# One more chunk in seven products: a two-stage kernel with its attention batches drawn closer together

## The chip, the cores and the metric

The kernel runs on one core of one Trainium2 chip. A core has engines that run side by side, each through its own list of instructions in order: TensorE (PE, matrix products, with PEld as its weight loads), VectorE (DVE), ScalarE (ACT), GpSimd (POOL) and SyncE (SP, which here only issues DMAs). They hand work to each other through semaphores. Data lies in SBUF (128 partitions), products land in PSUM banks, and sixteen DMA engines move data between memory and SBUF. The metric is the device time of one execution in microseconds; smaller is better.

## The reference

Four batches of linear attention with four heads come first (1088 positions, head size 32). Each query and key is turned into 64 features, all products of 8 by 8 sketch values:

```python
def phi(x):
    a = np.einsum('rd,bhsd->bhsr', S1, x)
    b = np.einsum('rd,bhsd->bhsr', S2, x)
    return np.einsum('bhsi,bhsj->bhsij', a, b).reshape(*x.shape[:-1], r * r)
q_p, k_p = (phi(q), phi(k))
kv = np.einsum('bhsf,bhsd->bhfd', k_p, v)
z = np.sum(k_p, axis=2)
num = np.einsum('bhsf,bhfd->bhsd', q_p, kv)
den = np.einsum('bhsf,bhf->bhs', q_p, z)[..., None] + 1e-06
```

num / den, reshaped to 4352 tokens of 128 values, is the input x of a gated layer with 1536 inner columns:

```python
gate = 1.0 / (1.0 + np.exp(-(x @ w_gate)))
val = x @ w_val
return (gate * val @ w_out).astype(np.float32)
```

All of it is float32. `z`, the sum of the key features over all positions, is what the text calls the feature sums.

## The kernel before, in words

Tokens are cut into eight chunks of 512 and a last one of 256. Weight columns are taken in blocks of 128, twelve for the gate, twelve for the value; w_out has twelve blocks of rows.

**Slots.** The first SECT = 5 chunks are worked in slots, twelve per chunk, numbered from 0 to 59. A slot (`slot`, line 745) does one wave (`w1`, line 667): the products of one gate block and one value block with 512 tokens, on TensorE; a sigmoid on ACT; and, one slot later, the gating product on DVE (`glu`, line 714). Some slots later come the products with w_out (`w2_a`, `w2_b`). Those use a form with seven products of half size where the plain one has eight, which needs sums of tokens (POOL, `token_sums`) and sums of weights. Two PSUM pairs serve the waves by turns, so TensorE can run about two waves ahead of the gating.

**Attention between slots.** Each batch is threaded through the slots by hand. For batches 2 and 3 the list `plan` (line 1468) says before which slot a step is issued: turning the raw keys and queries (`turn_k`, `turn_q`), `begin` (lines 1367 to 1371: sketch products, then the copies below), two outer products (`outer`), two steps of the feature sums (`sum_z`, line 1057), `kv_all`, a query multiplication (`qmult`) with `ndt`, the second query multiplication, and `parts` (line 1393), which ends the batch and makes its tokens ready. `parts` opens with `den_j` (line 1151), a TensorE product that reads the tile B8; a DVE product with A8 follows. Batch 1 goes through the same steps between slots 11 and 22.

**The copies.** `spread` (line 969) writes the compressed queries (cq) to a tile in DRAM called dq, through the ACT queue, and reads them back on the SP queue in repeated form. Six large reads fill QP and BQ: for each half of the tokens one of 576 KB (qp, source rows `[[8 * W1, 2 * R], [0, R]]`, so 16 outermost) and two of 288 KB (bq, source rows `[[0, R], [8 * W1, R]]`, so 8 outermost). Eight small reads of 32 partitions each follow and fill A8 and B8 (lines 991 to 1003, source `[[8 * W1, 32]] + run`). R is 8 and W1 is 288.

**Weights for the section.** `cross_weights` (line 463) prepares sums of weight halves in the tile fw. Its steps have letters, and `PREP` says after which slot each is done: DMAs between partition halves on ACT (v, w, x, y, z) and on SP (within d, e, n), subtractions and additions on DVE (d, e, s, f, g, t, u), one on ACT (n). X loads the section's first tokens, 0 and 2 form their sums on POOL.

**Section.** The last three full chunks and the chunk of 256 tokens follow in `section` (line 1498). There the first product too has seven products for eight, two blocks of columns by 256 tokens and half the depth at a time, with 64 x 64 quarters of TensorE side by side. Eighteen waves of this kind and the last chunk are issued in the order that the string `ORDER` spells out; a planner wrote it. In it P are feature products, W products with w_out, A, S, D and M the copies, sigmoids, additions and gating, Q and T sums on POOL, E and F the end of a chunk, C, Y, Z and O the last chunk. Two pairs of the last slot chunk (HELD) leave their w_out products to the section.

**Loads.** Raw k and q of a batch lie in one tile (`new_kq`), which later serves as BQ; `load_kq(b + 1)` refills it behind the second query multiplication of batch b, through SP.

Of the kernel before, what the change touches and what calls it, by code (L numbers as in the profile page):

```python
# [19 lines left out]
WUB:-2.0 P1:0 T0:1 P1':0 P5:1 P1':1 P5:0 P1:1 WLA:-2.1 Aa:0 P5':0 P5':1 Aa:1 P2':0 P6':0 P6:0 P2:0  # L20
Ac:0 P2':1 P6':1 Ac:1 D1:0 P2:1 P6:1 Sa:0 D1:1 P3:0 P7':0 P3':0 P7:0 T2:1 P7':1 P3:1 Sc:0 D2:0 P7:1
P3':1 Sa:1 P1:2 WUB:-1.0 D2:1 P5:2 P4':0 Sc:1 P1':2 P4:0 P4:1 P1:3 M1:0 P1':3 P4':1 P5:3 P5':2 Aa:2
M1:1 WUB:-1.1 WLA:-1.0 Ac:2 P6':2 WLA:-2.0 M2:1 P2:2 P6:2 Aa:3 P2':2 P5':3 Q0:1 D1:2 P6':3 P2':3
Ac:3 P6:3 P2:3 M2:0 Q1:1 P7':2 P3':2 Sa:3 P7:2 WLA:-1.1 D1:3 Q0:0 Sa:2 P3:2 P1:5 D2:2 P7:3 P3:3 Q2:1
Sc:2 P3':3 P7':3 P5:4 P4:2 T1:1 Sc:3 D2:3 P4':2 P1:4 Q3:1 P1':4 WUA:-2.0 M1:2 P5:5 P5':4 Q1:0 P1':5
P4':3 M2:2 Aa:4 WUA:-2.1 P4:3 Ac:4 Q2:0 P2:4 P6':4 M1:3 WLB:-2.0 P6:4 Q3:0 P2':4 WUA:-1.0 Aa:5 D1:4
WLB:-1.1 WUA:-1.1 P6:5 P5':5 M2:3 EA:-1 P7:4 P6':5 Sa:4 P3:4 P7':4 Q0:3 P3':4 P2:5 Ac:5 D2:4
WLB:-1.0 WUA:1.0 Q0:2 Sc:4 P1:6 P2':5 D1:5 P4':4 P1':6 EB:-1 T3:1 P4:4 P7':5 Sa:5 P3':5 P7:5 Q1:2
M1:4 WUA:1.1 P5':6 Q1:3 P1':7 P5:6 D2:5 Aa:6 P3:5 WLB:1.1 Ac:6 M2:4 P6':6 P2:6 Q2:3 P4:5 P6:6 Sc:5
P4':5 WUA:0.1 Q0:4 D1:6 WUA:0.0 WLB:1.0 Q3:3 P1:7 WLB:0.0 M1:5 P7:6 P3':6 M2:5 Q2:2 Aa:7 P7':6 P3:6  # L30
P2':6 P5:7 Sc:6 Q1:4 D2:6 P6:7 P5':7 P2':7 P6':7 F0:-1 Ac:7 T0:2 WLA:3.0 P2:7 WLA:0.0 P4':6 D1:7
Q3:2 Sa:7 P5':8 P4:6 M2:6 Sa:6 P5:8 WUB:1.1 Q2:4 P3':7 P7':7 M1:6 P3:7 P7:7 Q3:4 P1':8 P1':9 Sc:7
D2:7 P1:9 P1:8 Q0:5 Ac:8 WLA:0.1 WUB:0.0 P5:9 P4':7 Aa:8 M2:7 Q0:6 P4:7 WUB:3.0 WLA:3.1 WUB:1.0 Q1:5
M1:7 WLA:1.0 P6':8 WLA:2.1 P6:8 F1:-1 T2:2 Aa:9 P5':9 WLA:2.0 D1:8 WUB:2.0 WLA:1.1 Ac:9 WUB:3.1 P6:9
Q0:7 P7:8 P6':9 P7':8 P3:8 D1:9 Q1:7 P3':8 P2:9 P2':8 P2':9 D2:8 Q2:5 Sc:8 P3:9 P2:8 P3':9 P7:9 M2:8
Q1:6 Sa:8 P4':8 P7':9 Sc:9 P4:8 WLB:3.0 Q3:5 D2:9 WUA:2.0 WLB:2.0 Sa:9 WUA:2.1 WLB:3.1 M1:8 WUA:4.0
P4:9 Q0:8 M2:9 P4':9 P1:11 WUA:4.1 P1:10 Q1:8 M1:9 P1':10 P1':11 P5:11 P5':10 F2:-1 Q2:7 Aa:10 P5:10
WUA:3.0 F3:-1 Aa:11 WUA:3.1 WLB:5.0 Q3:7 F4:-1 P6:10 P2:10 Ac:10 P6':10 WLB:5.1 Q2:6 P6:11 P5':11
D1:10 WUA:5.0 WLB:4.0 Q0:9 Ac:11 WUA:5.1 P6':11 F5:-1 P7':10 P3':10 T1:2 D1:11 P7:10 P3:10 P2':11
P2':10 Q1:9 Sc:10 D2:10 P2:11 P7:11 Sa:10 P7':11 P3:11 T3:2 M2:10 P4:10 WLA:5.1 Sa:11 Q3:6 P4':10  # L40
WLA:5.0 D2:11 P3':11 WLA:4.0 Q2:8 WLA:4.1 WUB:4.0 M1:10 Sc:11 P4':11 WUB:5.1 EA:0 P4:11 WUB:5.0
M2:11 P1':13 P1:12 EB:0 P1:13 P1':12 M1:11 Q0:11 P5:13 P5:12 Aa:12 P5':13 P5':12 F6:-1 Q0:10 Aa:13
WUB:7.0 WLA:7.0 P6:12 WLA:6.0 Ac:12 Q1:10 P6':12 P6':13 Ac:13 WUB:7.1 P2:12 D1:12 Q2:10 P6:13
WUB:6.0 P2':13 WLA:7.1 F0:0 Q1:11 P7':12 P3:12 D1:13 P7:12 P3':12 Q3:10 WLA:6.1 P2:13 Sc:12 D2:12
P3':13 P2':12 Q2:11 P3:13 P7':13 M2:12 Sa:12 P7:13 P4:12 Q3:11 Sc:13 WLB:6.0 P4':12 D2:13 P1:14
WUA:6.0 Sa:13 Q3:8 WLB:7.1 WUA:6.1 M1:12 P4:13 P5':15 Q2:9 M2:13 P4':13 P1:15 WUA:7.0 P1':14 Q3:9
M1:13 WUA:7.1 WLB:7.0 Aa:14 P5:14 P1':15 Q0:12 F1:0 P5:15 P5':14 Aa:15 F2:0 P6:14 P2':14 Q0:13 Ac:14
P6':14 WLB:10.0 WLB:11.0 WUA:9.1 Q1:12 Ac:15 D1:14 WUA:8.1 P6':15 WUA:10.1 P6:15 F3:0 Q2:12 P7':14
P3':14 D1:15 P7:14 P3:14 P2:14 WUA:9.0 Sc:14 D2:14 WUA:10.0 WLB:11.1 Sa:14 WLB:9.1 WUA:11.0 M2:14
WLB:8.0 P4':14 WLB:9.0 P4:14 F4:0 P7:15 WUA:11.1 M1:14 P7':15 P3:15 WUA:8.0 P1':16 D2:15 P1:16  # L50
P3':15 P5':16 P2':15 F5:0 Sc:15 P5:16 P2:15 Aa:16 P4':15 WUB:9.1 P5':17 WLA:8.1 Sa:15 WUB:8.0
WLA:8.0 Ac:16 WLA:10.1 P6:16 M2:15 Q0:14 P6':16 P4:15 WLA:9.1 WUB:9.0 Q1:13 D1:16 P1':17 P2:16
WLA:9.0 P1:17 M1:15 Q3:12 P3:16 P7':16 Aa:17 P3':16 P7:16 Q0:15 WLA:10.0 P5:17 Sc:16 D2:16 WUB:10.0
WLA:11.1 Q2:13 Ac:17 WLA:11.0 P2':17 M2:16 P6':17 P2:17 Q3:13 EA:1 P4:16 P6:17 WUB:11.0 P2':16 Q1:15
D1:17 P4':16 WLA:12.0 Sa:16 Q1:14 WUB:11.1 WLA:13.0 Sa:17 P3':17 P7:17 M1:16 Q0:16 P7':17 P3:17 C1:1
Sc:17 D2:17 Q1:16 C0:1 C3:1 M2:17 Y:1 Q2:16 C2:1 EB:1 C0:0 Z:1 Q0:17 P4:17 WUA:13.0 WLB:13.1
WUA:12.0 Q2:14 F6:0 WLB:12.0 WUA:12.1 WLB:13.0 WUA:13.1 Q3:16 F0:1 C1:0 Q3:14 C2:0 F1:1 Y:0 C3:0
F2:1 Q2:15 C0:3 Z:0 C1:2 Q3:15 WUB:13.1 P4':17 WLA:13.1 WUB:12.0 M1:17 WUB:13.0 WLA:12.1 F3:1 C1:3
Q1:17 C2:3 F4:1 Y:3 C3:3 Q2:17 WFA:16.0 Z:3 WFA:14.0 Q3:17 WFA:15.0 WFA:16.1 F5:1 WFA:14.1 F6:1
WFA:15.1 WFA:17.0 WFA:17.1 C0:2 EA:2 WFB:15.0 WFB:17.1 WFB:17.0 WFB:16.0 Y:2 WFB:14.0 WFB:15.1 C2:2  # L60
EB:2 C3:2 F0:2 C1:5 C0:5 Z:2 O0:1 C3:5 C2:5 F1:2 Y:5 C0:4 Z:5 C1:4 C2:4 Y:4 C3:4 F2:2 O0:2 O0:3 Z:4
O1:5 O2:2 O2:1 O1:2 O3:3 F3:2 O3:5 O1:3 F4:2 O0:5 O2:0 O3:4 F5:2 O3:0 O1:0 O2:4 F6:2 O2:5 O1:4 O3:2
O0:0 O2:3 O3:1 O1:1 O0:4
# [4 lines left out]
def kernel(  # L68
# [23 lines left out]
    SECT, HELD = 5, 2  # L92
    PREP = (
        (22, "v"),
        (23, "dw"),
        (24, "ex"),
        (25, "s"),
        (26, "n"),
        (30, "f"),
        (32, "g"),  # L100
        (34, "t"),
        (37, "u"),
        (38, "y"),
        (39, "z"),
        (44, "X"),
        (45, "0"),
        (47, "2"),
# [355 lines left out]
    def cross_weights():  # L463
# [8 lines left out]
        (g0, g1), (v0, v1) = (turns(w_sb[:, k]) for k in range(2))  # L472
        (a0, a1), (b0, b1), (c0, c1) = (turns(fw[0][:, k]) for k in range(3))

        def sub(rows, out, x, y, op=ALU.subtract):
            nc.vector.tensor_tensor(out=out[rows], in0=x[rows], in1=y[rows], op=op)

        def cross(eng, out, x, rows):
# [17 lines left out]
            "u": lambda: sub(LO, b1, c1, a1),  # L496
            "y": lambda: cross(nc.scalar, a0, g0, LO),
            "z": lambda: cross(nc.scalar, a1, g1, HI),
            "X": lambda: load_y(0),
            "0": lambda: [x_sum(0, u) for u in (0, 1)],  # L500
            "2": lambda: [x_sum(0, u) for u in (2, 3)],
        }
        moe["prep"] += [(n, steps[k]) for n, ks in PREP for k in ks]

    def weight_sums(n0, n1):
        w = w_sb[:, 2].rearrange("p (n f) d -> p f n d", f=2)[:, :, n0:n1]
        s = ws[:, :, n0:n1]
        a11, a12 = w[:, 0, :, :64], w[:, 1, :, :64]
        a21, a22 = w[:, 0, :, 64:], w[:, 1, :, 64:]
# [935 lines left out]
    for pi in range(2):  # L1445
        outer(1, pi)
        slot(None, 1)
# [308 lines left out]
```

## Time and profile before

| what | value |
|---|---|
| median of three runs | 284.11 us (284.06 to 284.45) |
| profiled execution | 284.32 us, of which the span of its instructions is 282.5 us |
| granted TensorE clock | 1.000 |
| busy: PE, DVE, POOL, ACT | 276.7, 208.3, 179.7, 119.6 us |
| slots (sigmoid of slot 0 to that of slot 59) | 16.7 to 177.4 us |
| 50 to 178 us, busy DVE, POOL, ACT | 94.8, 85.9, 42.2 of 128 us |
| 178 to 253 us, busy DVE, POOL, ACT | 56.3, 56.1, 41.1 of 75 us |
| first den_j product of batch 1, 2, 3 | 71.89, 128.62, 170.31 us |

Positions in time are counted from the first instruction. In a row of instructions the columns are the start, the length, the engine, the line in the kernel, the operation, the output and inputs by their names in the program, and how many were merged. "SPq" and "ACTq" are instructions of an engine's queue that only issue something; a DMA's row gives the issue, and the data lands later. A float32 product shows as two records. For the waits, the engine and line come first, then who ended the wait, the sum in us, how often, and the longest. For stretches of time, the length is followed by each engine's busy time, the clock, the mean busy share of the sixteen DMA engines, and the rate in GB/s.

### The profile page before, as it was taken

Reading aid. Unit: us, or ns where it says so; the run is one execution under the profiler, and the core shown is the slowest. Engines: PE = TensorE matmul, PEld = TensorE weight load, DVE = VectorE, ACT = ScalarE, POOL = GpSimd, SP = SyncE. Lnnn points to the kernel's source line nnn. Section 1 sums busy time; section 2 is a strip of 40 time slices with the busy share of each in tenths; the row PEclk is TensorE's granted clock in tenths of the full one; section 3 lists DMA queues with packets and bytes.
Section 4 is the critical chain, followed back from the end, with each engine's and each line's share of the span. In section 5 each row is a group of like instructions: output and inputs, shape, how many; then the busy total and the mean of one; then the engine's idle time right before and its main releaser. Section 6 shows DMA issues by size and latency. Waiting matters only on the chain.

```text
span 282.5 us, 7859 instructions
## 1 busy us (share of the span) xinstructions
PE 276.7 (98%) x3204; PEld 158.6 (56%) x3204; DVE 208.3 (74%) x339; ACT 119.6 (42%) x232; POOL 179.7 (64%) x234
## 2 busy tenths in 40 slices
PE   8899999999999999999999999999999999999994
PEld 3554433354444444544444444577788888875674
DVE  6986789847687777786768857577788968579462
ACT  3689742322326222443225223666554554452130
POOL 2666674567575668664778765547798988197300
PEclk9999999999999999999999999999999999999999
DMA  7995540674681267376348520200310031003133
GB/s 210 334 372 144 119 157 15 167 155 138 198 182 43 41 179 151 95 151 182 74 130 155 134 45 15 64 0 18 89 25 2 2 71 19 2 21 66 24 64 57
DMA packets 33332, 29.02 MB, mean 103 GB/s; under 512 B 19216, under 2 KB 27728, under 8 KB 33296
## 3 DMA queue, kind: packets, MB, share of 16 engines
q1 hardware_dynamic: 28880, 25.44, 37.0%
q10 hardware_dynamic: 4416, 3.08, 4.2%
q8 instruction: 25, 0.41, 0.6%
q14 instruction: 11, 0.09, 0.1%
HBM read 20.60 MB, written 3.26 MB: 84 GB/s over the span
## 4 chain that ended last, share of the span: by engine, by line
PE 97%; ACT 1%; POOL 0%; DVE 0%; issue 0%
PE wave L682 37%; PE b L530 24%; PE prod L530 23%; PE moeout L574 4%; PE warm L379 2%; PE kvz L1027 1%; PE nps L1385 1%; PE kps L808 1%; PE moeout L530 1%; PE kvz L1014 1%; PE cqps L954 1%; PE nps L1217 0%; PE denj L1156 0%; PE nps L1169 0%; PE dps L1198 0%; ACT asb L925 0%
## 5 line engine op out<-in xcount | busy, mean ns | idle before, releaser
L682 PE MATMUL wave<-xT,w_sb 128*64 128x512 f32 (+2 forms) x436 | 117.5, 589 | 0.1
L530 PE MATMUL prod<-tsum,ws 64*64 64x256 f32 (+1 forms) x348 | 81.1, 379 | 0.0
L690 ACT ACTIVATE sg<-wave 128x512 f32<-128x512 f32 x60 | 35.8, 597 | 89.3 <-PE wave L682 85.2
L520 POOL TENSOR_TENSOR tsum<-g,tsum 128x256 f32<-128x256 f32 x48 | 47.2, 982 | 30.5 <-DVE g L717 30.2
L682 PEld LDWEIGHTS wave<-xT,w_sb 128*64 128x64 f32 (+1 forms) x436 | 40.0, 143 | 46.2 <-issue 35.9
L530 PE MATMUL b<-yt,fw 64*64 64x256 f32 x792 | 63.5, 378 | 0.0
L717 DVE TENSOR_TENSOR g<-wave,sg 128x512 f32<-128x512 f32 x60 | 41.1, 685 | 27.2 <-ACT sg L690 26.4
L530 PE MATMUL prod<-g,w_sb 64*64 64x256 f32 (+2 forms) x234 | 53.7, 377 | 0.0
L520 POOL TENSOR_TENSOR tsum<-g 128x256 f32<-128x256 f32 x48 | 40.4, 842 | 16.8 <-DVE g L717 16.5
L530 PEld LDWEIGHTS prod<-tsum,ws 64*64 64x64 f32 (+1 forms) x348 | 42.2, 135 | 11.0 <-issue 6.8
L530 PEld LDWEIGHTS b<-yt,fw 64*64 64x64 f32 x792 | 41.6, 133 | 9.6 <-DVE b L622 0.7
L1618 POOL TENSOR_TENSOR tsum<-g 128x256 f32<-128x256 f32 x36 | 28.8, 815 | 18.4 <-DVE g L1605 8.9
L530 PE MATMUL prod<-g,ws 64*64 64x256 f32 (+1 forms) x116 | 33.5, 377 | 0.0
L530 PEld LDWEIGHTS prod<-g,w_sb 64*64 64x64 f32 (+1 forms) x234 | 25.7, 135 | 13.6 <-issue 9.8
L530 PE MATMUL prod<-tsum,w_sb 64*64 64x256 f32 (+1 forms) x116 | 33.1, 379 | 0.0
L1618 POOL TENSOR_TENSOR tsum<-g,tsum 128x256 f32<-128x256 f32 x36 | 29.1, 819 | 1.1
L530 PE MATMUL b<-yt,w_sb 64*64 64x256 f32 x216 | 25.7, 377 | 0.0
L622 DVE TENSOR_TENSOR b<-b,s 128x512 f32<-128x512 f32 x18 | 12.5, 696 | 8.2 <-PE b L530 7.6
L1605 DVE TENSOR_TENSOR g<-c,sg 128x512 f32<-128x512 f32 x18 | 15.9, 886 | 3.5 <-PE prod L530 2.6
L530 PEld LDWEIGHTS prod<-g,ws 64*64 64x64 f32 (+1 forms) x116 | 15.6, 135 | 3.9
L530 PEld LDWEIGHTS b<-yt,w_sb 64*64 64x64 f32 x216 | 15.5, 133 | 2.4
L1597 ACT ACTIVATE sg<-b 128x512 f32<-128x512 f32 x18 | 10.8, 598 | 14.4 <-PE b L530 14.0
(162 smaller groups left out, 380.4 us busy)
## 6 DMA issues: line engine op xcount, KB each, us to landing
qp<-dq SPq DMA_DIRECT2D x7, 576.0 KB, 5.3
bq<-dq SPq DMA_DIRECT2D x14, 288.0 KB
kq<-in_k_dram SPq DMA_DIRECT2D x3, 544.0 KB
kq<-in_q_dram SPq DMA_DIRECT2D x3, 544.0 KB
w_in<-in_moe_w_out_dram SPq DMA_DIRECT2D x6, 256.0 KB
yt<-xT SPq DMA_DIRECT2D x12, 128.0 KB
w_in<-in_moe_w_gate_dram SPq DMA_DIRECT2D x5, 256.0 KB, 6.7
w_in<-in_moe_w_val_dram SPq DMA_DIRECT2D x5, 256.0 KB, 4.7
```

The lines of the kernel that those rows point to most:

```text
L379: nc.tensor.matmul(out=t[:, 0, :n], lhsT=x, rhs=r, start=True, stop=True)
L520: nc.gpsimd.tensor_tensor(out=t[:, u], in0=in0, in1=in1, op=ALU.subtract)
L530: nc.tensor.matmul(out=out, lhsT=lhsT, rhs=rhs, start=start, stop=stop, skip_group_check=True)
L574: nc.tensor.matmul(out=moe["acc"][d], lhsT=w_sb[:, 2, j, d], rhs=g[:, jj], start=(j == 0), stop=(j == NJ - 1),)
L622: nc.vector.tensor_tensor(out=out, in0=in0, in1=in1, op=ALU.add)
L682: nc.tensor.matmul(out=wv[d, which, jj * tw + o : jj * tw + o + tp], lhsT=w_sb[:, which, j0 + jj, d], rhs=xT[:, t0 + o : t0 + o + tp], sta ...
L690: nc.scalar.activation(out=sg, in_=wv[:, 0], func=ACTF.Sigmoid)
L717: nc.vector.tensor_tensor(out=g, in0=wv[:, 1], in1=sg, op=MUL)
L808: nc.tensor.matmul(out=ts[pi][32 * g : 32 * g + 32, : NJK * 32], lhsT=sk[rows, :], rhs=kT_of[b][rows, KBASE[g] : KBASE[g] + NJK], start=Tr ...
L1597: nc.scalar.activation(out=sg[:, :, second], in_=two(gc), func=ACTF.Sigmoid)
L1605: nc.vector.tensor_tensor(out=g[:, :, second], in0=two(c2), in1=sg[:, :, second], op=MUL)
L1618: nc.gpsimd.tensor_tensor(out=t[:, out], in0=in0, in1=in1, op=ALU.subtract)
```

## The change

Chunk 4 moves from the slots to the section: SECT is 4, there are 48 slots, and the section has 24 waves of seven-product form and a new ORDER. So that the attention is done in time:

- Batches 2 and 3 have new places: their steps run from before slot 25 to slot 34 and from before slot 37 to slot 46.
- Batch 3's raw k and q are loaded into tiles of their own through the ACT queue, as steps K, P and Q of PREP behind slots 27, 28 and 29; the `load_kq` at the end of a batch is gone.
- `cross_weights` is called between batch 1's outer products, and PREP starts at slot 14. Two of its DVE steps (t, u) have counterparts on POOL (T, U) that take their place.
- The feature sums are two reductions on DVE over eight blocks of positions; the ninth block, of 64 partitions, is added by four more small products in `kv`. The tile z4 of the sums is no longer needed for them.
- A8 and B8 are read by six DMAs of 64 partitions: two for A8 and one for B8 in each half, with `[2 * W1, 2], [8 * W1, 32]` as the source's rows.

```diff
-    SECT, HELD = 5, 2
+    SECT, HELD = 4, 2
     PREP = (
-        (22, "v"), (23, "dw"), (24, "ex"), (25, "s"), (26, "n"), (30, "f"), (32, "g"),
-        (34, "t"), (37, "u"), (38, "y"), (39, "z"), (44, "X"), (45, "0"), (47, "2"),
+        (14, "v"), (15, "w"), (16, "x"), (17, "de"), (19, "s"), (20, "n"), (23, "f"),
+        (24, "y"), (25, "U"), (27, "K"), (28, "P"), (29, "Q"), (32, "g"), (33, "z"),
+        (35, "T"), (34, "X"), (37, "0"), (41, "2"),
     )
...
+            "T": lambda: sub(every, b0, v0, b0, ALU.add, nc.gpsimd),
+            "U": lambda: sub(LO, b1, c1, a1, eng=nc.gpsimd),
...
+        kx = fwp.tile([P, T, D], F32, tag="kx", name="kx")
+        k_t[3] = kx
+        q_t[3] = [fwp.tile([P, T0, D], F32, tag="qx", name="qx")]
+
+        def load_x(n):
+            t0, tn = (0, T) if n < 0 else (2 * q_chk[n][0], 2 * q_chk[n][1])
+            if n == 1:
+                q_t[3].append(sbA.tile([P, tn, D], F32, tag="z4", name="qx1", bufs=1))
+            src, t = (k, kx) if n < 0 else (q, q_t[3][n])
+            nc.scalar.dma_start(
+                out=t,
+                in_=bass.AP(
+                    tensor=src.tensor, offset=src[3, 0].offset + t0 * D, ap=[[T * D, P], [1, tn * D]]
+                ),
+            )
+
+        steps["K"] = lambda: load_x(-1)
+        steps["P"] = lambda: load_x(0)
+        steps["Q"] = lambda: load_x(1)
...
+        d0, d1 = d[0, 0], d[2, 0]
         for x in range(2):
-            for m in range(2):
-                p0 = 64 * x + 32 * m
-                for i, t in enumerate((A8[b], B8[b])):
-                    d0 = d[2 * i + m, 0]
-                    if i == 0:
-                        offset, run = d0.offset + (W1 - WD) * x, [[W1, 2], [1, WD]]
-                    else:
-                        offset, run = d0.offset + W1 * x, [[1, W1]]
-                    put.dma_start(
-                        out=t[p0 : p0 + 32],
-                        in_=bass.AP(tensor=d0.tensor, offset=offset, ap=[[8 * W1, 32]] + run),
-                    )
+            rows = slice(64 * x, 64 * x + 64)
+            for c in range(2):
+                put.dma_start(
+                    out=A8[b][rows, c],
+                    in_=bass.AP(
+                        tensor=d0.tensor,
+                        offset=d0.offset + W1 * c + (W1 - WD) * x,
+                        ap=[[2 * W1, 2], [8 * W1, 32], [1, WD]],
+                    ),
+                )
+            put.dma_start(
+                out=B8[b][rows],
+                in_=bass.AP(
+                    tensor=d1.tensor, offset=d1.offset + W1 * x, ap=[[2 * W1, 2], [8 * W1, 32], [1, W1]]
+                ),
+            )
...
-        for h in range(H):
-            nc.tensor.matmul(
-                out=kvz[32 * h : 32 * h + 32, F : 2 * F],
-                lhsT=nc.const_aps.tensor(1.0, [P, 32], F32),
-                rhs=zsum[:, h, :],
+        for n, rhs in ((P, lambda h: zsum[:, h, :]), (64, lambda h: KP[b][:64, h // 2, 0, h % 2, :])):
+            for h in range(H):
+                nc.tensor.matmul(
+                    out=kvz[32 * h : 32 * h + 32, F : 2 * F],
+                    lhsT=nc.const_aps.tensor(1.0, [P, 32], F32)[:n],
+                    rhs=rhs(h),
...
-        kp = KP[b].rearrange("p c j m f -> p c j (m f)")
...
+        kp = KP[b].rearrange("p c j m f -> p c (m f) j")[:, step]
         if step == 0:
-            Z4[b] = sbA.tile([P, 2, 4, 2 * F], F32, tag="z4", name="z4", bufs=1)
-            add(Z4[b], kp[:, :, 1:5], kp[:, :, 5:9])
-            return
-        z4 = Z4[b]
-        add(z4[:, :, :2], z4[:, :, :2], z4[:, :, 2:])
-        ZS[b] = sbA.tile([P, H, F], F32, tag="zs", name="zs", bufs=1)
-        zc = ZS[b].rearrange("p (c m) f -> p c (m f)", c=2)
-        add(zc, z4[:, :, 0], z4[:, :, 1])
-        add(zc[:64], zc[:64], kp[:64, :, 0])
+            ZS[b] = sbA.tile([P, H, F], F32, tag="zs", name="zs", bufs=1)
+        nc.vector.tensor_reduce(
+            out=ZS[b][:, 2 * step : 2 * step + 2].rearrange("p m f -> p (m f)"),
+            in_=kp[:, :, 1:],
+            axis=mybir.AxisListType.X,
+            op=ALU.add,
+        )
...
         outer(1, pi)
+        if pi == 1:
+            cross_weights()
...
-    plan = {2: (27, 29, 30, 31, 32, 34, 36, 37, 38, 39, 41, 43)}
-    plan[3] = (46, 47, 47, 47, 49, 50, 51, 53, 54, 55, 57, 58)
+    plan = {2: (25, 26, 26, 26, 28, 29, 30, 31, 31, 32, 34, 34)}
+    plan[3] = (37, 38, 38, 38, 40, 41, 42, 43, 43, 44, 46, 46)
...
         qmult(b, 1)
-        load_kq(b + 1)
```

The new ORDER string, of the same kind with 24 waves, is not shown.

## The prediction

> **What bounds the kernel now.** I read the page from the top: busy times, then the slices, then the chain that ended last.
>
> ```profile
> PE 276.7 (98%) x3204; PEld 158.6 (56%) x3204; DVE 208.3 (74%) x339; ACT 119.6 (42%) x232; POOL 179.7 (64%) x234
> PEclk9999999999999999999999999999999999999999
> DMA  7995540674681267376348520200310031003133
> PE 97%; ACT 1%; POOL 0%; DVE 0%; issue 0%
> ```
>
> TensorE is the chain, at full granted clock, and from 15 us on it hardly waits. So two questions matter: how much TensorE work goes, and what new wait TensorE meets. The prices of the work are in the pieces of the chain (start, length, records):
>
> ```profile
> 142.31 1.72 PE wave L682 x8
> 212.09 3.24 PE b L530 x60
> ```
>
> A slot's whole first product is 8 records in 1.72 us; in the section a run of feature products takes 3.24/60 = 0.054 us a record.
>
> The second question is one of DMA. Batch 3's copies of the compressed queries, as the queues issued them, and the product that needs the last of them:
>
> ```profile
> 142.29 0.35 ACTq L972 DMA_DIRECT2D dq<-cq  x1
> ...
> 144.47 0.55 SPq L979 DMA_DIRECT2D qp<-dq  x1
> 145.12 1.27 SPq L979 DMA_DIRECT2D bq<-dq  x2
> ...
> 149.75 0.31 SPq L1000 DMA_DIRECT2D a<-dq  x1
> 152.28 0.31 SPq L1000 DMA_DIRECT2D b<-dq  x1
> ...
> 162.57 0.31 SPq L1000 DMA_DIRECT2D b<-dq  x1
> ...
> 170.31 0.50 PE L1156 MATMUL denj<-b,zw 64*32 64x160 f32 x16
> ```
>
> The small copies a and b (A8, B8) are issued in steps because each waits for an older DMA; the SP queue's waits say so:
>
> ```profile
> SPq L1000 <- DMA bq<-dq: 9.1, 4, 2.9
> SPq L1000 <- DMA qp<-dq: 2.6, 2, 2.1
> ```
>
> Read together, the ninth copy goes out when the first has landed (149.75), the last when the sixth, the second half's last bq, has (162.57). That is 20.3 us after the write of dq was issued. How the engines were filled meanwhile (after the window: its length, busy times, clock, DMA share, GB/s):
>
> ```profile
> 146.00:152.00 6.00, 6.00 (x40) 2.72 (x38) 5.04 (x7) 2.32 (x5) 5.92 (x6) 1.00 0.97 203
> 154.00:161.00 7.00, 7.00 (x120) 3.66 (x118) 6.90 (x11) 2.78 (x6) 4.44 (x6) 1.00 0.57 136
> 126.40:130.40 4.00, 4.00 (x68) 1.73 (x66) 1.99 (x4) 1.32 (x3) 3.07 (x5) 1.00 0.97 305
> 81.00:85.00 4.00, 4.00 (x30) 1.92 (x28) 2.88 (x4) 1.59 (x4) 3.52 (x4) 1.00 1.02 249
> ```
>
> In the first window all sixteen DMA engines work, in the second only 0.57 x 16 = 9 of them, though copies are still queued. qp's source pattern has 16 rows outermost, bq's has 8. [...]
>
> **The change part by part.** The sum is made against the profiled execution: 284.3 us, of which 282.5 are the span; the median of the runs shown is 0.2 lower.
>
> One chunk moves from slots to section. Its first product costs 12 x 1.72 = 20.6 us in slots. In the section it is six waves of 28 products, two records each: 336 x 0.054 = 18.1. Both places use the seven-product form for the second matmul, so that stays. **-2.5 us**, all on TensorE's path.
>
> kv gets four more products per batch, eight records, for the block left out of the feature sums. The same group of 24 records for three batches is 0.9 us busy now, kv's other 216 are 3.6 us (0.4 for 24). I take **+0.5**.
>
> The feature sums go from four VectorE additions (1.42, 0.86, 0.84, 0.83 us a batch) to two reductions of 1,024 elements. Reductions of 128 elements took 0.27 us along memory and 0.37 across it, of 64 elements 0.22 and 0.26; by the slopes one new reduction costs 1.0 to 1.9 us, two 2.0 to 3.9. VectorE gains 0 to 1.9 us a batch. It sits beside TensorE, so 0. If VectorE became the limit this would be a gain; it does not: between begin and parts of batches 2 and 3 it has some 20 us of work (nine gates at 0.69, two outer products at 1.43, the sums, two multiplications of 2.7 together, the transposes and one chunk's additions) in 8 slots of about 25 us.
>
> Two preparations of the feature weights (T, U) move to POOL. 192 columns took 0.59 us and 256 took 0.72, so 768 are about 1.8 us each. POOL has 17 to 23 of 28 us busy in the stage, and they stand where only one token sum is due in front of them: 0, at most 1.8 once. The section's six more waves find DVE and POOL at 56 of 75 us: 0. The weight crossings come nine slots earlier; their four SP issues now stand behind batch 1's copies, but the first reader (f, slot 23) comes behind batch 1's parts anyway: 0. On SP the next chunk's store and v loads queue behind batch 2's copies, and v is read twelve slots on: 0. ACT gets three issues for batch 3's raw q and k where SP loses two, some 0.4 us each; ACT has 18 of 28 us idle: 0 as time on ACT.
>
> Now the distances. Batch 3 goes from begin to parts in 8 slots where it took 11, batch 2 in 8 where it took 12; batch 1 keeps 10. Four slots are 9.95 us (sigmoids at 146.44 and 156.39), 2.49 each. From the dq issue to den_j it was 170.31 - 142.29 = 28.0 us in batch 3, and will be 20.5; batch 2: 128.62 - 98.03 = 30.6, will be 20.6; batch 1 stays at 71.89 - 48.40 = 23.5.
>
> What has to land by then? The last bq landed 20.3, 20.9 and 19.4 us after dq in batches 3, 2 and 1 (162.57, 118.89, 67.80, from the same kind of row). Behind it come A8 and B8: 4 x 40 KB and 4 x 36 KB on the page, 311 thousand bytes. Now their eight sources have 32 rows outermost. The six new ones have **two** outermost ([2*W1, 2], then 32 rows). [...] Nothing in this trace has an outermost 2, so bounds. A busy engine moved 305/(0.97 x 16) = 19.7 GB/s in the raw loads and 136/(0.57 x 16) = 14.9 in the bq stretch; the third slice's 372 GB/s at nine tenths or more makes at most 25.8. On two engines that is 6.0, 7.9 or 10.4 us. On sixteen it is 1.0, on eight (the nearest row, bq) 2.0 to 2.6. I take two engines at 19.7 GB/s, 7.9 us, because the step from 16 to 8 followed the outermost count, and the raw loads, like these, read each row once.
>
> TensorE runs in order, so den_j holds every wave behind it (the second query multiplication waits for bq in the same moment, and is covered by this):
> - batch 3: 20.3 + 7.9 - 20.5 = **+7.7**
> - batch 2: 20.9 + 7.9 - 20.6 = 8.2. Batch 3's raw loads (1.11 million bytes, 3.6 us at 305 GB/s) are issued one to three slots behind begin(2), into the same engines. Between nothing and 3.6 I take half: **+10.0**
> - batch 1: 19.4 + 7.9 - 23.5 = 3.8. Three crossings of 192 KB now fall in its copies, 2.4 us at 249 GB/s; half again: **+5.0**
>
> Sum: 284.3 - 2.5 + 0.5 + 22.7 = 305.0; against the median **304.8**. At 25.8 GB/s with loads and crossings free it is 296, at 14.9 with both in full 315.
>
> [...]
>
> **The rivals.**
> *The copies stay spread.* Then A8 and B8 land about 1 us behind bq, as now (the copy issued at 149.75 took 13.5 us, to 163.3, 21.0 behind dq). Batches 3 and 2 are late by 0.5 and 1.0 us, raw loads add up to 3.6: 284.1 - 2.0 + 1.5 + 1.8 to 3.6 = 286. For it: nothing shows an outermost 2. Against: the 0.57.
> *The gain arrives.* As before, but raw loads slip into idle engines, and with all twelve copies issued by the fourth landing instead of the sixth the tail shrinks to some 0.5 us: 284.1 - 2.0 + 0.7 = 282.8, faster. The point that decides is when A8 and B8 land: with a summed lateness under 1.4 us it is faster. For it: TensorE's saving is certain. Against: 20.3 and 20.9 leave no room even now.
> *ACT is held too.* The waits above are on DMAs eight back. If ACT's crossings and raw loads share that count, ACT stands at an issue until bq or A8 lands, and sigmoids stop. Much of that is the same wait; up to 10 us is not: 308 to 320. For it: ACT issues in order in front of the next sigmoid. Against: its five crossings in the old place show no such wait.
>
> **How the numbers follow.** Forecast 0.70 (296 to 315, likeliest 305), ACT held 0.06, copies spread 0.10, gain 0.14. 0.2% is about what a measurement can tell from no change. Faster: 0.14 and 0.02 of the spread case; same 0.03; slower 0.81. The range runs from 284, leaving out the gain, to 315.
>
> **What would show it.** In the new profile: six issues at the A8/B8 lines, none in step behind the last bq; a stretch behind it with a DMA share near 0.13 (2 of 16); denj idle before, released by DMA b, some 5, 10 and 8 us; 96 wave records fewer and 336 more of b, at the old prices. If the share stays at a half and denj waits under 1 us, the reading of the outermost count is wrong and the time is 282 to 287. A sigmoid idle behind an ACT DMA issue would show the third rival.

## The result and the profile after

The changed kernel takes **313.36 us** (median of 4 runs, 312.60 to 314.67) against 284.13 of the kernel before on the same chip (4 runs): ratio **1.103**, 95% interval 1.099 to 1.108. The time lies in the forecast range; it is 8.6 us over the likeliest value of the sum, 304.8. The profiled execution took 312.61 us, its span 310.8. From here on, differences are made between profiled executions (312.6 - 284.3 = 28.3 us) unless medians are named.

The page of the kernel after: the row of TensorE, its granted clock in 40 slices, and the chain's shares by engine.

```profile
PE 282.9 (91%) x3552; PEld 185.6 (60%) x3552; DVE 214.9 (69%) x344; ACT 124.3 (40%) x239; POOL 177.2 (57%) x240
...
PEclk9999999998599999699997999999999999999999
...
PE 69%; DMA 20%; SPq 5%; DVE 2%; ACT 1%; issue 1%; POOL 0%; DVEq 0%
```

TensorE was 97% of the chain; now a quarter of it is DMA and the SP queue. And the granted clock, which had been 1.0 throughout, has three dents. TensorE's waits (in all, times, longest) say where:

```profile
PE denj L1195 <- DMA b<-dq: 17.0, 6, 5.2
PE b L569 <- ACT b L1630: 1.7, 1, 1.7
PE kvz L1081 <- DVE zs L1106: 1.2, 2, 0.6
```

den_j waits for b (B8), as forecast: 7.4 us in batch 1 (2.22 and 5.15, for B8's two halves), 6.4 in batch 2 (3.04 and 3.31), 3.2 in batch 3 (0.30 and 2.95). That makes 17.0 us; an expectation below counts 16.7, without the 0.30. The other two rows were not forecast. The chain through batch 3's copies (start, length, what):

```profile
141.17 2.09 DMA dq<-cq
...
143.31 5.12 DMA qp<-dq
...
148.45 6.91 SPq L1042
...
156.43 3.33 SPq L1034
...
159.80 6.96 DMA b<-dq
```

and how the engines stood in that stretch (length, busy times of PE, PEld, DVE, ACT and POOL, then clock, DMA share, GB/s):

```profile
160.00:162.00 2.00, 2.00 (x16) 0.91 (x14) 1.19 (x3) 0.60 (x1) 1.74 (x3) 1.00 0.14 45
162.00:164.00 2.00, 1.56 (x14) 0.33 (x10) 1.21 (x1) 0.60 (x1) 1.77 (x1) 1.00 0.25 59
164.00:166.00 2.00, 0.00 (x0) 0.00 (x0) 0.00 (x0) 0.00 (x0) 0.00 (x0) 1.00 0.48 94
```

0.14 x 16 is 2.2 engines. In the trace's packets, from 160 to 162 us all data is in packets of 640 and 1,152 bytes (the rows of A8 and B8), and for 80% of that time exactly two of them are under way. The trace does not name the engine of a packet, but the same count bears out the prediction's reading of bq: in the kernel before, from 154 to 161 us, exactly eight of its packets of 4,608 bytes are under way for 81% of the time. From 162.2 us a store's packets of 128 bytes come beside them, which is why the share rises while A8 and B8 go on at the old pace: 256 + 128 packets, 311 thousand bytes, from 17.6 to 25.1 us behind the write of dq. That is 7.5 us, 41.5 GB/s, or 20.8 for each of two under way.

Now the clock. The trace's record of it has, in order, full clock for 71.68 us, half for 10.24, full for 37.55, half for 6.83, full for 37.55, half for 3.41 and full for 139.95: 21, 3, 11, 2, 11, 1 and 41 times 3.413 us. The wait of batch 1 in windows of that length, cut where the granted clock changed:

```profile
72.16:75.57 3.41, 0.48 (x8) 0.15 (x8) 1.24 (x2) 0.60 (x1) 1.95 (x2) 1.00 0.40 99
75.57:78.99 3.42, 0.00 (x0) 0.00 (x0) 0.00 (x0) 0.00 (x0) 0.00 (x0) 0.50 1.04 214
78.99:82.40 3.41, 2.39 (x40) 1.26 (x40) 1.09 (x2) 0.00 (x0) 0.33 (x1) 0.50 0.67 137
82.40:85.81 3.41, 3.41 (x28) 1.91 (x22) 2.24 (x6) 1.01 (x1) 1.76 (x3) 0.50 0.93 287
85.81:89.23 3.42, 3.42 (x23) 1.39 (x21) 3.22 (x6) 0.60 (x1) 0.52 (x1) 1.00 0.39 88
```

TensorE is released at 80.01 and works at half clock until 85.81. The same happens from 125.15 to 130.19 and from about 167.7 to 171.15. Work takes twice as long there: pairs of products with 256 columns (L569) started every 0.42 us from 83.11 to 84.38 and, at full clock, every 0.21 us from 160.34 to 160.98. So 5.8, 5.0 and 3.4 us lose 2.9, 2.5 and 1.7: by this estimate **7.1 us** behind the waits that no term of the forecast held.

What held the copies back in batches 1 and 2 is in the SP queue's waits:

```profile
SPq L1034 <- DMA fw<-w_sb: 11.5, 2, 9.5
...
SPq L1034 <- DMA kx<-in_k_dram: 6.0, 1, 6.0
...
SPq L1034 <- DMA bq<-dq: 4.8, 2, 2.8
```

SP's issues of A8 (L1034) wait for the weight crossings (fw) and batch 3's raw k (kx), which ACT issued. No tile is common to A8 and these transfers. But the two queues share the semaphores that their DMAs signal: in the trace's records the 188 issues name eight, each named 23 or 24 times, 1 to 5 of them by ACT. The issue of A8 at 68.34 us waits for the one that the crossing issued at 53.55 signals, last at 68.32; the issue at 113.41 waits for that of kx, issued at 100.99, which signals last at 113.39. In batch 3 no such wait stands; there two issues themselves took 6.91 and 3.33 us (the SPq rows of the chain), and why is not shown.

### The profile page after: what moved, and what is told of

It is laid out like the page before. It is cut to its first block, busy times and chain, and to the rows that moved or that the text cites. A ratio compares the mean times of both kernels' runs of the same rounds, so it can differ in the third digit from the quotient of the medians.

```text
span 310.8 us, 8592 instructions
## 1 busy us (share of the span) xinstructions
PE 282.9 (91%) x3552; PEld 185.6 (60%) x3552; DVE 214.9 (69%) x344; ACT 124.3 (40%) x239; POOL 177.2 (57%) x240
## 4 chain that ended last, share of the span: by engine, by line
PE 69%; DMA 20%; SPq 5%; DVE 2%; ACT 1%; issue 1%; POOL 0%; DVEq 0%
PE b L569 26%; PE wave L721 16%; PE prod L569 16%; DMA b<-dq 7%; DMA fw<-w_sb 5%; DMA qx<-in_q_dram 4%; PE moeout L613 3%; SPq L1034 2%; SPq L1042 2%; PE nps L1424 2%; DMA qp<-dq 2%; PE kps L847 1%; PE moeout L569 1%; DMA s_in<-in_S_dram 1%; PE nps L1208 1%
## 5 line engine op out<-in xcount | busy, mean ns | idle before, releaser
L721 PE MATMUL wave<-xT,w_sb 128*64 128x512 f32 (+2 forms) x340 | 94.4, 593 | 0.2
L569 PE MATMUL prod<-tsum,ws 64*64 64x256 f32 (+1 forms) x384 | 92.9, 386 | 0.0
L569 PE MATMUL b<-yt,fw 64*64 64x256 f32 x1056 | 88.4, 377 | 1.7 <-ACT b L1630 1.7
L569 PEld LDWEIGHTS b<-yt,fw 64*64 64x64 f32 x1056 | 62.1, 133 | 6.4 <-ACT b L1630 2.4
L729 ACT ACTIVATE sg<-wave 128x512 f32<-128x512 f32 x48 | 28.7, 597 | 74.9 <-PE wave L721 72.9
L559 POOL TENSOR_TENSOR tsum<-g,tsum 128x256 f32<-128x256 f32 x36 | 32.3, 896 | 44.3 <-DVE g L756 41.7
L569 PE MATMUL prod<-g,w_sb 64*64 64x256 f32 (+2 forms) x258 | 57.2, 382 | 0.0
L721 PEld LDWEIGHTS wave<-xT,w_sb 128*64 128x64 f32 (+1 forms) x340 | 32.9, 149 | 39.3 <-issue 30.4
L569 PEld LDWEIGHTS prod<-tsum,ws 64*64 64x64 f32 (+1 forms) x384 | 49.3, 137 | 7.2 <-issue 4.6
L756 DVE TENSOR_TENSOR g<-wave,sg 128x512 f32<-128x512 f32 x48 | 32.9, 685 | 18.5 <-ACT sg L729 18.5
L559 POOL TENSOR_TENSOR tsum<-g 128x256 f32<-128x256 f32 x36 | 29.6, 821 | 22.8 <-DVE g L756 22.3
L569 PE MATMUL prod<-g,ws 64*64 64x256 f32 (+1 forms) x128 | 37.5, 389 | 0.0
L1657 POOL TENSOR_TENSOR tsum<-g,tsum 128x256 f32<-128x256 f32 x48 | 36.5, 773 | 1.2
L569 PE MATMUL prod<-tsum,w_sb 64*64 64x256 f32 (+1 forms) x128 | 36.7, 379 | 0.0
L569 PEld LDWEIGHTS prod<-g,w_sb 64*64 64x64 f32 (+1 forms) x258 | 27.6, 136 | 10.7 <-issue 7.2
L569 PE MATMUL b<-yt,w_sb 64*64 64x256 f32 x288 | 33.3, 376 | 0.7 <-DVE c L661 0.7
L661 DVE TENSOR_TENSOR b<-b,s 128x512 f32<-128x512 f32 x24 | 16.7, 698 | 13.5 <-PE b L569 12.6
L1636 ACT ACTIVATE sg<-b 128x512 f32<-128x512 f32 x24 | 14.3, 599 | 19.8 <-PE b L569 19.8
L569 PEld LDWEIGHTS b<-yt,w_sb 64*64 64x64 f32 x288 | 19.3, 133 | 2.3 <-POOL tsum L1657 1.1
L569 PEld LDWEIGHTS prod<-g,ws 64*64 64x64 f32 (+1 forms) x128 | 17.6, 139 | 3.6 <-issue 1.1
```

Source lines behind the costliest of these rows:

```text
L559: nc.gpsimd.tensor_tensor(out=t[:, u], in0=in0, in1=in1, op=ALU.subtract)
L569: nc.tensor.matmul(out=out, lhsT=lhsT, rhs=rhs, start=start, stop=stop, skip_group_check=True)
L661: nc.vector.tensor_tensor(out=out, in0=in0, in1=in1, op=ALU.add)
L721: nc.tensor.matmul(out=wv[d, which, jj * tw + o : jj * tw + o + tp], lhsT=w_sb[:, which, j0 + jj, d], rhs=xT[:, t0 + o : t0 + o + tp], sta ...
L729: nc.scalar.activation(out=sg, in_=wv[:, 0], func=ACTF.Sigmoid)
L756: nc.vector.tensor_tensor(out=g, in0=wv[:, 1], in1=sg, op=MUL)
```

## The experiments

The theory: A8 and B8 run on two DMA engines because two is the outermost count of their new form; that alone makes den_j wait, loads and crossings beside the copies make it worse, and the waits pull the clock down. Below, "two engines" means two packets under way at a time. The main rival: the traffic and the late issues are the cause, and the form of the copies is not. Four runs make a square of the two. In kernels in which den_j waits, executions differ by some us; I give the median and the range.

### New copies alone, in the kernel before

In `spread` of the kernel before, only this:

```diff
-        for x in range(2):
-            for m in range(2):
-                p0 = 64 * x + 32 * m
...
-                        in_=bass.AP(tensor=d0.tensor, offset=offset, ap=[[8 * W1, 32]] + run),
+        for x in range(2):
+            rows = slice(64 * x, 64 * x + 64)
...
+                    in_=bass.AP(
+                        tensor=d1.tensor, offset=d1.offset + W1 * x, ap=[[2 * W1, 2], [8 * W1, 32], [1, W1]]
+                    ),
```

> The kernel before, with only the six new copies of A8 and B8 per batch (two outermost); slots, loads and crossings stay where they were. Theory (two engines): in the kernel after, batch 3, with no other traffic, has its last copy 25.6 us behind the write of dq. Batch 1 of the kernel before has 23.5 us, batches 2 and 3 have 30.6 and 28.0: den_j of batch 1 waits 1 to 4 us, and a fall of the clock adds 1 to 2; the others wait nothing. 285.5 to 290 us, with a stretch at a DMA share near 0.13 in each batch. Rival (not the engines but late issues and traffic): 283.8 to 284.5 us.

Measured: 290.77 us (288.41 to 291.84), ratio 1.022 (1.017 to 1.027); the median is 0.8 us above the bounds. TensorE's wait in it:

```profile
PE denj L1161 <- DMA b<-dq: 4.7, 1, 4.7
```

One wait, in batch 1, as expected, 4.7 us where the bound was 4, followed by 3.4 us at half clock (1.7 us lost, by the same estimate). Batches 2 and 3 show the slow copies without paying for them. Batch 3's stretch behind the last bq:

```profile
168.00:170.00 2.00, 2.00 (x16) 0.86 (x14) 0.71 (x1) 0.10 (x1) 1.99 (x3) 1.00 0.19 57
```

Before, the last A8/B8 packet of batch 3 ended 21.6 us behind the write of dq; here 25.2, with the last bq at 18.2. In the window shown, two packets of A8 and B8 are under way for 82% of the time (other transfers make up the rest of the share); in the old form, from 161.9 to 163.9 us of the kernel before, up to 13 are. No slot and no load was moved, so the form of the copies is the cause. The rival "not the form" (284 us) is out. The edit changes three things at once, the number of the copies, the rows of each and the outermost count. The number is not it: the run "Half of it on two engines" has six copies as well, and its den_j waits less. Rows and outermost count were not varied apart; that it is the count rests on the packets, two at a time here and eight for bq, whose copies have 64 rows too.

### Old copies, in the kernel after

The reverse of the diff above.

> The kernel after, with the eight copies of A8 and B8 per batch in their old form (32 rows outermost); all else stays. Theory (the copies run on two DMA engines): den_j's 16.7 us of waiting fall to 1 to 3, since the copies land about 1 us behind the last bq again; without the long waits the granted clock stays at 1.0, which returns the 7.1 us at half clock. 313.4 - 16.7 - 7.1 + 1 to 3 = 289 to 293 us. Rival (the late issues at shared semaphores and the crossings and raw loads beside the copies are what is late, not the number of engines): more than half of the waiting stays, 300 us or more.

Measured: 295.07 us (291.67 to 296.87; the profiled one is 296.87), above the bounds in the median and inside them in the lowest execution; the rival's 300 is not reached. 18 of the 29 us between the medians are gone, but not all of den_j's waits:

```profile
PE denj L1190 <- DMA b<-dq: 5.4, 4, 2.8
```

2.0 us in batch 1, 3.4 in batch 2, none in batch 3, where the last packet now ends 20.6 us behind dq. In batches 1 and 2 the last bq packets end at 22.2 and 22.8 us, against 18.4 and 19.8 before: that is the traffic. And the clock fell here too, though no single wait is long:

```profile
72.09:75.51 3.42, 1.45 (x28) 0.61 (x32) 1.49 (x2) 0.60 (x1) 0.72 (x1) 1.00 0.41 83
75.51:78.92 3.41, 3.41 (x43) 1.95 (x29) 2.08 (x5) 1.01 (x1) 2.09 (x3) 0.50 0.96 231
```

The first window has two idle gaps, of 0.57 and 1.40 us, and is 0.42 busy; the next was granted 0.5. My expectation, that the clock would stay up, was wrong.

### New copies, loads and crossings moved away

```diff
-        (14, "v"),
-        (15, "w"),
-        (16, "x"),
+        (10, "v"),
+        (10, "w"),
+        (10, "x"),
...
+        (24, "KPQ"),
...
-        (27, "K"),
-        (28, "P"),
-        (29, "Q"),
...
     turn_k(1)
+    cross_weights()
     slot(None, 1)
...
-        if pi == 1:
-            cross_weights()
```

> The kernel after, with its new copies, but nothing else moved beside them: the three crossings v, w, x issued in the slot ahead of batch 1's begin instead of slots 14 to 16, batch 3's three raw loads in slot 24 instead of 27 to 29. Theory (two engines are the base of it, the traffic an addition): batch 3 keeps its wait of 3 us, batches 1 and 2 fall from 7.4 and 6.4 to 2 to 4 us each, with a shorter stretch at half clock: 313.4 - 7 - 2 = 302 to 306 us. Rival 1 (the traffic is all of it): batches 1 and 2 wait nothing, 295 us or less. Rival 2 (the traffic costs nothing): 313 us.

Measured: 305.77 us (302.14 to 307.78), in the bounds. den_j:

```profile
PE denj L1193 <- DMA b<-dq: 10.2, 3, 3.6
```

3.60, 3.62 and 2.95 us by batch. The last bq of batches 1 and 2 lands 18.5 and 18.9 us behind dq instead of 22.4 and 21.1. So the traffic costs 2 to 4 us of landing time in those two batches, but without it the new copies are still late in all three. Each wait is followed by a stretch at half clock, 3.4 us long in batches 1 and 2.

### Both undone

The old copies and the moved loads together.

> The kernel after with both earlier edits together: the eight copies of A8 and B8 in their old form, and crossings v, w, x and batch 3's raw loads moved out of the copies' time. Theory (two engines, plus the traffic that adds to them): in batch 3 of the run with the old copies the last one ended 20.6 us behind the write of dq, and den_j comes 20.6 (batches 2 and 3) to 23.5 us (batch 1) behind it. So den_j waits under 1 us in every batch, no stretch has a granted clock of 0.5, and what is left above the kernel before is kv (about 1.9 us by the slots) and two waits of the section (2.3 us), less the moved chunk (3.3 us): 285 to 286.5 us. Rival (distances alone are too short, whatever the copies): den_j still waits 2 us or more in batches 2 and 3, 289 us or more.

Measured: 287.52 us (286.55 to 288.73), ratio 1.012 (1.010 to 1.015); 1 us above the bounds, the profiled execution (286.55) at their edge. No wait of den_j, clock 1.0 throughout. What TensorE still waits for:

```profile
PE kvz L1074 <- DVE zs L1099: 1.2, 2, 0.6
PE b L567 <- ACT b L1622: 0.8, 1, 0.8
...
PE b L567 <- DVE c L659: 0.7, 1, 0.7
```

The square, in medians (us):

| | loads and crossings beside the copies | moved away |
|---|---|---|
| new copies | 313.4 | 305.8 |
| old copies | 295.1 | 287.5 |

In the medians the copies are worth 18.3 us in both columns and the traffic 7.6 in both rows. That the two agree so well is chance: executions in the two cells with only one edit spread over 5 us and more, and with the middle of their two lowest (303.5 and 292.8) the copies are worth 16.0 and 20.6 us, the traffic 9.9 and 5.3. The sum does not depend on it: together they are 25.8 of the 29.2 us between the corners. The remaining 3.4 are neither.

### Half of it on two engines

The kernel with the moved loads, A8 back in its old form (32 rows outermost), B8 in the new one.

```diff
-            for c in range(2):
+            for m in range(2):
+                dm = d[m, 0]
                 put.dma_start(
-                    out=A8[b][rows, c],
+                    out=A8[b][64 * x + 32 * m : 64 * x + 32 * m + 32],
...
-                        ap=[[2 * W1, 2], [8 * W1, 32], [1, WD]],
+                        ap=[[8 * W1, 32], [W1, 2], [1, WD]],
```

> The run with moved loads and new copies, but A8 (164 KB) copied in its old form with 32 rows outermost, only B8 (147 KB) by two copies with two outermost. Theory (what has two outermost moves at the 41 GB/s that 311 KB in 7.5 us make): B8's packets need 3.6 us, so the last lands about 18.3 + 3.6 = 21.9 us behind the write of dq, batch 3's den_j (20.5) waits 1.4 us, batch 2's 1.5 to 2.0, batch 1's (23.5) nothing. A wait of 1.4 to 2.0 us leaves each window of 3.413 us busy at least 0.42: the clock may stay at 1.0. 287.5 + 3 = 289 to 292 us. Rival (the share of the copies with two outermost does not matter): 287 to 288 us or 305 us.

Measured: 294.79 us (288.39 to 296.38), above the bounds; the profiled execution took 295.43. One execution lies some 6 us under the others, so the time itself decides little; what follows is read from the packets. In batch 3 B8's packets run from 19.2 to 23.1 us behind dq, 3.9 us for 147 thousand bytes (3.6 forecast), and den_j waits 1.34 us (1.4 forecast); in batch 2 it waits 1.64. So in batch 3 half of the bytes in the two-outermost form took half of the 7.5 us. The miss is batch 1, where I expected no wait: 1.75 us and half clock from 75.19 to 78.60. Bytes of A8 still came at 22.2 us behind dq there; what was in their way I did not isolate.

### TensorE kept busy through the wait

```diff
         t = ps2.tile([P, 2, 512], F32, tag="two", name="denj")
+        for i in range({1: 8, 2: 7, 3: 3}[b]):
+            nc.tensor.matmul(
+                out=t[:, i % 2],
+                lhsT=w_sb[:, 2, 0],
+                rhs=w_sb[:, 2, :4].rearrange("p j d -> p (j d)"),
+                start=True,
+                stop=True,
+            )
```

> The kernel after, with 8, 7 and 3 products of 512 columns that nobody reads (into the tile that den_j then overwrites) ahead of den_j in batches 1, 2 and 3, so that TensorE works through most of the wait. Theory (the granted clock falls because TensorE stands idle, and needs some us of work to come back): den_j is released at the same moments, but the 7.1 us at half clock behind it go: 306 to 307 us. Rival (the clock falls for another cause, the DMA traffic or the sections themselves): half clock stays, 313 us or a little more.

Measured: 310.24 us (309.30 to 311.93), between the two expectations; the profiled execution 309.41, 3.2 less than 312.61. In it the half clock is gone (in the other three the granted clock was 0.991 to 0.993, against 0.967 in every execution of the kernel after):

```profile
PEclk9999999999999999999999999999999999999999
```

Extra work on TensorE made the kernel faster. It is 3 us and not 7 because the copies landed later here: from the write of dq to den_j's release it was 32.6, 32.0 and 25.8 us against 32.0, 28.7 and 25.6. Batch 2's 3.3 us are the most of it. What delayed its copies I did not find; SP stood 7.0 us at the second issue of A8 there, 6.0 in the kernel after. den_j still idled 3.46 us in batch 2, and the clock stayed up:

```profile
120.98:124.39 3.41, 1.73 (x12) 0.41 (x10) 0.00 (x0) 0.00 (x0) 0.00 (x0) 1.00 0.52 106
124.39:127.81 3.42, 1.64 (x44) 0.89 (x46) 1.09 (x2) 0.19 (x1) 0.00 (x0) 1.00 0.73 164
127.81:131.22 3.41, 3.41 (x27) 1.72 (x25) 2.98 (x7) 1.37 (x2) 2.12 (x3) 1.00 0.36 77
```

The gap lies across two windows and leaves them 0.51 and 0.48 busy. So in these runs the clock does not go with the length of a gap.

### The feature sums and kv alone, in the kernel before

`kv` and `sum_z` of the kernel after in the kernel before; nothing else.

> The kernel before with only the new feature sums (two reductions) and kv's four more products a batch; slots as before, so that the second reduction stands a slot ahead of kv. Theory (the 0.6 us that kv waits for the second reduction in batches 2 and 3 of the kernel after come from the plan, which puts both into one slot, and the products themselves cost little): 284.3 to 284.9 us, with no wait of kvz for zs. Rival (the reductions, 1.95 us each where the four additions took 3.95 together, are late whatever the plan): 285.3 us or more.

Measured: 285.15 us (285.00 to 285.47), ratio 1.004 (1.003 to 1.005): 1.1 us, between the two expectations. kvz waits for no sum here, so the waits of the kernel after come from its plan. The added products are 0.9 us busy (then the mean in ns and the idle time before them):

```profile
L1037 PE MATMUL kvz<-kp,const-float32-1.0 64*32 64x64 f32 x24 | 0.9, 228 | 0.0
```

They overlap with others: TensorE's whole busy time grew by 0.5 us (277.2 against 276.7). So the products are the likely cost, but 0.6 of the 1.1 us is not placed.

### Can the rest be taken back?

Four versions on top of "both undone". The first: kv a slot behind the second sum, batches 2 and 3 spread over one slot more, and in the section the first store behind the late copies (F6:0 behind EB:1).

```diff
-    plan = {2: (25, 26, 26, 26, 28, 29, 30, 31, 31, 32, 34, 34)}
-    plan[3] = (37, 38, 38, 38, 40, 41, 42, 43, 43, 44, 46, 46)
+    plan = {2: (25, 26, 26, 26, 28, 29, 30, 31, 32, 33, 35, 35)}
+    plan[3] = (36, 37, 37, 37, 39, 40, 41, 42, 43, 45, 47, 47)
```

> As the run with old copies and moved loads, and besides: parts of batches 2 and 3 in slots 35 and 47 instead of 34 and 46 (batch 3 begins in 37 instead of 38), kv one slot behind the second reduction, and in the section the store of its first chunk (eight DMAs on SP) behind the three copies of the next chunk's second half instead of ahead of them. Theory: no wait of den_j, none of kvz for zs, none in the section for the late copies; what remains is the moved chunk's saving of about 3.3 us against kv's 0.7: 281.5 to 283 us, faster than the kernel before. Rival (another wait takes the place of the section's or of kv's): 284 us or more.

Measured: 290.23 us (287.00 to 290.67), far above the theory's 283. The rival's case: the waits aimed at are gone, and three others stand in their place.

```profile
PE b L565 <- issue: 1.5, 1, 1.5
PE kps L843 <- DVE kT L812: 1.5, 1, 1.5
PE cqps L989 <- DVE qT L823: 1.1, 1, 1.1
```

Batch 3's transposes now stand on VectorE right behind batch 2's parts, and the section right behind batch 3's. Behind the two waits for kT and qT the clock was 0.5 as well, from 119.53 to 122.94 us.

The second keeps begin and parts where they were (26, 34, 38, 46) and adds the left-out block on VectorE:

```diff
+    plan = {2: (25, 26, 26, 26, 28, 29, 30, 31, 32, 33, 34, 34)}
+    plan[3] = (37, 38, 38, 38, 40, 41, 42, 43, 44, 45, 46, 46)
...
+        if step == 1:
+            zc = ZS[b][:64].rearrange("p (c m) f -> p c (m f)", c=2)
+            k0 = KP[b].rearrange("p c j m f -> p c j (m f)")[:64, :, 0]
+            nc.vector.tensor_tensor(out=zc, in0=zc, in1=k0, op=ALU.add)
```

> As the run with old copies and moved loads (profiled execution 286.6 us), with three edits more: kv of batches 2 and 3 one slot behind the second reduction (the begin and parts of each batch stay in slots 26, 34, 38 and 46); the block left out of the feature sums added on VectorE by one addition on 64 partitions instead of four products more in kv; the section's store of its first chunk behind the next chunk's three late copies. Theory: each takes back what its own run or trace shows, 1.2 us (kvz waiting for zs, twice 0.61), 1.1 us (the products, from the run with the sums alone) and 1.5 us (two waits in the section): 286.6 - 3.8 = 282.8, 282.3 to 283.5 us, faster than the kernel before. Rival (a wait moves on, as the late transposes did in the earlier replanned run): 284 us or more.

Measured: 285.31 us (283.76 to 287.68), ratio 1.003 (1.000 to 1.005); the profiled execution 284.45. The time is the rival's, above the theory's 283.5. All four aimed-at waits are gone, 0.8 us came back at the second query multiplication:

```profile
PE nps L1418 <- DVE qp L1042: 0.8, 2, 0.4
```

TensorE's busy time is 2.2 us less here than in the kernel before (274.5 against 276.7), and it idles as much more; 0.8 of that is this wait.

That the store was the section's wait shows in what moved. In the kernel after, the SP queue had (start, length):

```profile
248.13 5.35 SPq L581 DMA_DIRECT2D out_dram<-o_sb  x8
253.57 0.47 SPq L1671 DMA_DIRECT2D xb<-e  x1
254.09 0.59 SPq L1672 DMA_DIRECT2D xb<-e  x1
```

Eight store issues held the copies xb, on which VectorE's additions and then the banks of the next products waited. With the store behind them TensorE waits for none of it.

Two more tried whether a batch still came late in those executions of the second that took longest: batch 3 a slot earlier (`plan[3] = (36, 37, 37, 37, 39, 40, 41, 42, 43, 44, 45, 46)`), and parts of batch 2 in slot 35.

> The second replanned run (profiled execution 284.5 us, but executions up to 285.8) with batch 3 one slot earlier: transposes from slot 36, begin in 37, second query multiplication in 45, parts still in 46. Theory: that run's spread comes from executions in which the last copies, 20.1 us behind the write of dq in batch 3 of the profiled one, come later than den_j (about 20.6); with some 23 us for batch 3 they are never late, and the wait of 0.4 us on the second query multiplication goes: 283.0 to 284.5 us, with a narrower spread. Rival (batch 2 is the one that comes late, or the earlier transposes wait): as the second replanned run, 284.5 to 286 us.

> The second replanned run with parts of batch 2 in slot 35 instead of 34 (its second query multiplication stays in 34); batch 3 as there. Theory: batch 2, whose copies share the engines with v's loads, is the one that comes late in the slower executions; with one slot more it is not, and its wait of 0.4 us on the multiplication goes: 283.0 to 284.5 us. Rival (batch 3 is the late one, or its transposes behind parts wait): 284.5 to 286 us.

Measured: 283.95 us (283.32 to 287.13), ratio 0.999 (0.996 to 1.002), and 284.50 us (283.95 to 287.84), ratio 1.003 (1.000 to 1.006). The first fits its theory, but a narrower spread is not shown (one execution at 287.13); the second lies where its two expectations meet and settles nothing. So the change with its copies and its plan mended equals the kernel before; a gain over it is not shown.

## Why the prediction was right, and where it was off

The sign, the place (den_j, on DMA b) and the cause (two outermost, two engines) held; the likeliest time was 8.6 us low. Step by step:

**Two engines, 7.9 us.** Right: 7.5 us in the quiet batch, 20.8 GB/s for each of two packets under way where 19.7 was taken for an engine. No run shows by name that two engines carry these copies; the packets show two under way for 80% of the time, at a share of 0.14. The nearest row alone, bq on eight engines, would have given some 288: 305.0 less 5.6 us a batch (7.9 against 2.0 to 2.6).

**Waits of 7.7, 10.0 and 5.0 us.** Sum 22.7, measured 17.0; each is off. *Batch 3* (3.2): bq's last packet came 18.3 us behind dq, not 20.3. The row I used is the issue that waited for bq, 0.9 us later than the packet; and with A8 and B8 no longer among them bq itself ended sooner. And TensorE reached den_j 21.9 us behind dq, not 20.5, because the slots taken out are shorter (2.17, 2.59, 2.16) than the mean of 2.49 and kv's became longer. *Batch 2* (6.4): the same two errors, and half of the raw loads, 1.8 us, was near: the last bq came 2.2 us later than with the loads moved. *Batch 1* (7.4): the term for the crossings, half of 2.4 us, was too small. bq's last packet came at 22.4 against 18.5 with the crossings moved, 3.9 us; from there to den_j's release it took 9.6 us where batch 3 took 7.3, while SP stood at the issues of A8. Counted in full the crossings would have been 2.4 us; the cost was larger still.

**ACT held at the shared count.** The rival named a mechanism that the waits fit, in the wrong direction: it is SP's issue that waits for ACT's transfers, up to 9.5 us; ACT's longest such wait is 2.0 us. The sign that no issue stands in step behind the last bq failed for that reason in batches 1 and 2; in batch 3 the last issue too came only when bq had landed (159.80), behind the two long issues.

**What had no term: the clock.** 7.1 us. I counted a wait at its length. The run with extra products holds the clock at 1.0, though its copies landed 4.1 us later in sum; so a wait on DMA cost TensorE here its length and, by the estimate above, 1.7 to 2.9 us more.

**kv +0.5, feature sums 0.** The sums and products alone cost 1.1 us (median), of which 0.5 shows as busy time of TensorE. The sums' duration was at the upper end of its bounds (1.95 us each, two 3.9), but their cover failed: the plan has the second sum and kv in one slot, and kv waits 0.6 us twice. I had named VectorE's total load, not the distance from the second sum to its reader.

**Chunk -2.5.** Near: in the three last versions, whose kv has no extra products, TensorE is busy 274.5, 274.0 and 275.5 us against 276.7 before, in the mean 2.1 us less. But the section lost 2.4 us to waits that the term had at nothing. I had looked at DVE and POOL there, not at SP, on which a store of eight issues now stood in front of xb.

In sum, against 305.0: clock +7.1, den_j -5.7, kv and sums +1.8, section +2.4, chunk +0.4 make 311.0; the measured execution is 312.6. About 1.6 us I could not place. That the two largest errors, the clock left out and den_j's waits taken too long, nearly cancelled is luck: with the waits as they were and no clock the sum would have been 299. The range was wide enough for either, since it went from the highest to the lowest speed read for an engine (25.8 and 14.9 GB/s).

## What to carry to other kernels

Read the outermost count of a DMA's pattern before merging several DMAs into fewer: six issues instead of eight cost some 18 us here with the clock behind the waits, because 2 x 32 rows moved two packets at a time where copies of 32 rows had up to 13 under way. Price a wait of TensorE on DMA at its length plus the half clock behind it (here 1.7 to 2.9 us more, by the estimate above), and count what an edit puts beside it in the same queue and engines, and which transfers of another queue its issues wait for. A result needed by the next instruction of another engine is not "hidden beside it", however idle its engine is: kvz waited 0.6 us twice for the second sum.

## What was not expected of the hardware

The granted clock is 1.0 or 0.5 here. In the kernel after, the stretches at half clock last 10.24, 6.83 and 3.41 us, and all that lie inside the span change at whole multiples of 3.413 us from one another; in the views of the old copies, the new copies alone, the first replanned version and half on two engines, a stretch at half clock lasts 3.4 us each time. In the rows below the clock of a window goes mostly with how busy TensorE was in the one before (busy as the profile models it). These are the windows at which the two outcomes lie nearest to each other, and some others:

| kernel, window start | busy share | clock in it | clock of the next |
|---|---|---|---|
| after, 72.16 | 0.14 | 1.0 | 0.5 |
| old copies, 72.09 | 0.42 | 1.0 | 0.5 |
| first replanned, 116.11 | 0.42 | 1.0 | 0.5 |
| half on two engines, 71.78 | 0.49 | 1.0 | 0.5 |
| TensorE kept busy, 124.39 | 0.48 | 1.0 | 1.0 |
| TensorE kept busy, 120.98 | 0.51 | 1.0 | 1.0 |
| after, 78.99 | 0.70 | 0.5 | 0.5 |
| first replanned, 119.53 | 0.82 | 0.5 | 1.0 |

Of these windows at full clock, those 0.14, 0.42, 0.42 and 0.49 busy were followed by half clock, those 0.48 and 0.51 busy by full clock, so the busy share as modelled does not part them sharply; of the two at half clock, the one 0.70 busy was followed by half clock and the one 0.82 busy by full clock. The length of a gap does not part them either: behind gaps of 0.57 and 1.40 us in one window (old copies) the clock was 0.5, behind a gap of 3.46 us across two (TensorE kept busy) it was 1.0.
